# Output matrix in 8 KB runs of head pairs, and halves of a key pair joined ahead of the gather, in a decode step on one core

## The chip, the core and the metric

The kernel runs on one core of a Trainium2 chip. The core has a matrix engine (TensorE, PE in the profile, with PEld for its weight loads), a vector engine (DVE), a scalar engine (ACT), GpSimd (POOL) and a sync engine (SP) that issues nearly all of the loads. Sixteen DMA engines move data between HBM and the on-chip memory (SBUF). [...] The metric is device time of one execution in microseconds; the numbers of the profile come from one profiled execution.

## The reference

One decode step of a layer for 8 batch rows (B) of width 512 (D): a layer norm, attention with 32 query heads that share 8 key/value heads over the last 1024 positions of a 4096-long cache, and beside it a GELU-gated feed-forward of width 1792, whose silu gates the attention's output.

```python
xn = _layernorm(x)
q  = (xn @ wq)                                  # 32 heads of 128
k, v = last 1024 positions of the caches        # 8 heads, each for 4 query heads
scores = einsum("bhqd,bhkd->bhqk", q, k) * 128 ** -0.5
o  = einsum("bhqk,bhkd->bhqd", softmax(scores), v)
s  = o.reshape(B, 1, 4096) @ wo                 # the output matrix, 4096 x 512
g  = silu((gelu(xn @ w_gate) * (xn @ w_up)) @ w_down)
return x + s * g
```

All inputs are bf16. Keys and values of the window are 16 MB each, wq and wo 4 MB each, the feed-forward's three matrices 1.8 MB each: 47.5 MB in all.

## The kernel before, in words

**Loads.** Every large load goes through SP's queue into one pool of nine buffers of 2 MB (`big`, line 71): wq, the gate and up matrices, then keys (K) and values (V), a 2 MB tile for each of the 8 key heads, then the output matrix. `pending` (line 548) fixes the order K0 K1 K2, down, V0 K3 V1 K4 and so on to K7 V5 V6 V7; `fetch` issues them. A load waits on SP until PE has done with the buffer that it takes. `load_wo` (line 127) loads the output matrix in five pieces (lines 623 to 626): heads 0 to 3, heads 4 and 5, head 6, three quarters of head 7, the last quarter. Row `4p + r` of a head's 512 rows goes to partition p, so a head gives each partition one run of 4 rows, 4 KB.

**Sets.** A set is four batch rows of one key head: 16 sets (NS), two for each head (NB = 2). In a set each partition holds 32 consecutive keys of one batch row. The keys lie in pairs, and a pair (256 values in bf16) is turned as 128 four-byte words. For a set the kernel does, in order: `transpose_quarter` four times (four PE transposes each; one quarter is copied out by DVE, line 444, the next by ACT, line 446); `scores` (line 450), whose DVE step also finds each row's largest; `maxima` (line 471), a PE matmul into the columns `m_top` of a bank and a DVE step that makes the bias of the exponential; `exponentials` on ACT (line 485), which also sums; `turn` (line 496), a transpose on DVE; `value_half` twice (line 504); and for each head `gather` (line 520).

**The output of a set.** `value_half` multiplies 16 chunks of turned probabilities by pairs of values. Both keys of a pair meet the same weight columns, so the result (128 x 2 x 128, in the one bank of `ps_o`) holds for each row two halves, and only one of them is meant for it: `half` (line 261) says which. ACT copies both halves into `blk` (line 516), a 129th column of which holds the sum from the exponential; POOL copies that column for the second half (line 492). `gather(h)` sums over partitions with four PE matmuls for a head (two sets, two halves; the masks `sums`, lines 286 to 295, have `half` worked in) into the columns `m_out` of the bank that `m_top` also lies in, divides by the sum (DVE lines 531 and 533) and transposes the head into `oL` (line 541), the left operand of the projection. `project` (line 609) multiplies `oL` by the output matrix's rows, 16 matmuls a head, into one accumulator.

**The order.** The main loop (line 571) has two half-steps for a set, `t = 2s + i`. Each issues, for several sets at once: exponentials of set s-2, transposes of set s, the gather, more transposes, `turn` of s-2, scores or maxima of s-1, and a half of the values of the set nine half-steps behind. The engines take their instructions in this order, each from its own queue, so an instruction that waits holds up all behind it on that engine. The gather of head h comes at `i == 1` with `s = 6 + 2h`: after the first quarter's transposes, and ahead of that half-step's `maxima`. A set's values end at an even t, and its ACT copy comes at the end of that half-step. After the last gather come the 128 projection matmuls, in the order of the pieces, then two DVE steps and the two output DMAs.

Of the kernel before, what the change touches and what calls it, by code (L numbers as in the profile page):

```python
# [8 lines left out]
ACT = mybir.ActivationFunctionType  # L9
ALU = mybir.AluOpType  # L10
AX = mybir.AxisListType
BF16 = mybir.dt.bfloat16
FP32 = mybir.dt.float32
# [4 lines left out]
def kernel(  # L18
# [13 lines left out]
    nc = tc.nc  # L32

    B, Sq, D = A_x.shape
    Hkv, Sk, Dh = A_k_cache.shape[1], A_k_cache.shape[2], A_k_cache.shape[3]
    Hq = A_wq.shape[1] // Dh
    rep = Hq // Hkv
# [5 lines left out]
    scale = float(Dh) ** -0.5  # L43
    P = nc.NUM_PARTITIONS
# [6 lines left out]
    G = 4  # L51
    NB = B // G
# [4 lines left out]
    SET = NCH * Dh  # L57
# [3 lines left out]
    DP = Dh // 2  # L61
    NQB = D // 128
    PB = 32 // B

    NG = 2
    NS2 = NQB // NG
# [4 lines left out]
    big = ctx.enter_context(tc.tile_pool(name="big", bufs=9))  # L71
    kT_pool = ctx.enter_context(tc.tile_pool(name="kT_pool", bufs=2))
    p_pool = ctx.enter_context(tc.tile_pool(name="p_pool", bufs=2))
    consts = ctx.enter_context(tc.tile_pool(name="consts", bufs=1))
    small = ctx.enter_context(tc.tile_pool(name="small", bufs=3))
# [9 lines left out]


    m_ps = ps_m.tile([P, 512], FP32, name="m_ps")
    m_top, m_out = m_ps[:, 0:P], m_ps[:, P : P + Dh + 1]


    x_sb = rows.tile([B, D], BF16, name="x_sb")
# [23 lines left out]
                nc.sync.dma_start(out=t[:, y, :], in_=src[y])  # L115
        return [t[:, y, :].rearrange("p (c d) -> p c d", c=NCH) for y in range(NB)]

    HB = 2 * SET // (rep * D)
    wo_tiles = {}

    def wo_at(h):

        if h // HB not in wo_tiles:
            wo_tiles[h // HB] = big.tile([P, HB, rep * D], BF16, name="big")
        return wo_tiles[h // HB]

    def load_wo(h, r0, n, nh=1):

        t = wo_at(h)[:, h % HB : h % HB + nh, r0 * D : (r0 + n) * D]
        nc.sync.dma_start(  # L130
            out=t if nh > 1 else t[:, 0, :],
            in_=A_wo[h * rep * Dh : (h + nh) * rep * Dh, :].rearrange(
                "(h p r) n -> p h (r n)", p=P, r=rep
            )[:, :, r0 * D : (r0 + n) * D]
            if nh > 1
            else A_wo[h * rep * Dh : (h + 1) * rep * Dh, :].rearrange(
                "(p r) n -> p r n", r=rep
            )[:, r0 : r0 + n, :],
        )
        return [t[:, i, :].rearrange("p (r n) -> p r n", r=n) for i in range(nh)]  # L140

    wq_rows = []
    for k0, cuts in ((0, (1, 1)), (2, (2,))):
        t = big.tile([P, 2, Hq * Dh], BF16, name="big")
        i = 0
# [93 lines left out]
    quarter = consts.tile([P, NS2 + 32], FP32, name="quarter")  # L239
    nc.gpsimd.memset(quarter, 0.0)  # L240
    gsel = lead.tile([P, G], FP32, name="gsel")
    sums = consts.tile([P, 2, 2, rep, B, PB], FP32, name="sums")
    nc.gpsimd.memset(sums, 0.0)
    qT = qT0.rearrange("p (e s c g j) -> p e s c g j", e=2, c=2, g=G, j=rep)


    OW = 32
    OL = rep * OW
    oL = rows.tile([P, NS2 * (Hkv + 1), OL + 1], BF16, name="oL")
    nc.gpsimd.memset(oL, 0.0)  # L250

    def masks():
        nc.vector.tensor_reduce(
            out=parts, in_=identf.rearrange("p (x n) -> p n x", n=NC),
            axis=AX.X, op=ALU.max,
        )
        nc.vector.tensor_reduce(
            out=gsel, in_=parts.rearrange("p (g j) -> p g j", j=rep),
            axis=AX.X, op=ALU.max,
        )  # L260
        nc.vector.tensor_reduce(
            out=half, in_=identf.rearrange("p (r c n) -> p c r n", c=2, n=NC),
            axis=AX.XY, op=ALU.max,
        )
        nc.vector.tensor_reduce(
            out=quarter[:, NS2 : NS2 + B * NS2 : NS2],
            in_=identf.rearrange("p (a b f) -> p f b a", b=B, f=PB)[:, 0],
            axis=AX.X, op=ALU.max,
        )

        nc.vector.tensor_scalar(
            out=gsel, in0=gsel, scalar1=-1.0, scalar2=-NEG, op0=ALU.add, op1=ALU.mult
        )
        nc.vector.tensor_copy(
            out=own.rearrange("p c b g -> p (c b) g"),
            in_=gsel.unsqueeze(1).to_broadcast([P, CP * 32 // G, G]),
        )

        m = small.tile([P, NC], FP32, name="m16")
        nc.vector.tensor_scalar(  # L280
            out=m, in0=parts, scalar1=-1.0, scalar2=-NEG, op0=ALU.add, op1=ALU.mult
        )
        nc.vector.tensor_copy(
            out=same, in_=m.unsqueeze(1).to_broadcast([P, NR * 2, NC])
        )
        for c in range(2):
            for b in range(2):
                nc.vector.tensor_scalar(
                    out=sums[:, c, b].rearrange(
                        "p j (g y) f -> p y j g f", y=NB  # L290
                    )[:, b],
                    in0=parts.rearrange("p (g j) -> p j g", j=rep)
                    .unsqueeze(3).to_broadcast([P, rep, G, PB]),
                    scalar1=half[:, c : c + 1], scalar2=None, op0=ALU.mult,
                )

    hT = rows.tile([P, NFC, 32], BF16, name="hT")
# [7 lines left out]
    for k in range(NDC):  # L305
        w = wq_rows[k]
        for t in range(NT):
            for g in range(NQB):
# [3 lines left out]
                    w[:, 0, h * HD : (h + 1) * HD],  # L312
                    start=(k == 0), stop=(k == NDC - 1), skip_group_check=True,
                )
    q_row = rows.tile([P, NT, rep, 2, 2, DP], BF16, name="q_row")
    for c in range(2):
        nc.vector.tensor_copy(  # L317
            out=q_row[:, 0, :, :, c, :],
# [91 lines left out]

    def fold():

        f_sb = rows.tile([P, D], FP32, name="f_sb")
        nc.scalar.activation(out=f_sb, in_=f_state["ps"], func=ACT.Copy)
        spread(m_top, quarter, f_sb)
        f_state["ps"] = m_top[0 : 32 * NG]
# [66 lines left out]
        biases[s] = bias  # L483

    def exponentials(s):
        blk[s] = small.tile([P, 2, Dh + 1], FP32, name="blk", bufs=6)
        P_[s] = p_pool.tile([P, CP * 32], BF16, name="p")
        nc.scalar.activation(  # L488
            out=P_[s], in_=sc.pop(s), func=ACT.Exp, scale=scale, bias=biases.pop(s),
            accum_out=blk[s][:, 0, Dh : Dh + 1],  # L490
        )
        nc.gpsimd.tensor_copy(  # L492
            out=blk[s][:, 1, Dh : Dh + 1], in_=blk[s][:, 0, Dh : Dh + 1]
        )

    def turn(s):
# [2 lines left out]
            out=pT[s].rearrange("p c k -> p (c k)"), in_=P_.pop(s)  # L499
        )  # L500

    o_ps = {}

    def value_half(s, i):
        if i == 0:
            o_ps[s] = ps_o.tile([P, 2, Dh], FP32, name="o_ps")
        for c in range(i * CP // 2, (i + 1) * CP // 2):
            q = c % NR
            nc.tensor.matmul(  # L509
                o_ps[s][32 * q : 32 * q + 32].rearrange("p c d -> p (c d)"),  # L510
                pT[s][:, c, :],
                V[s][:, 2 * c : 2 * c + 2, :].rearrange("p c d -> p (c d)"),
                start=(c < NR), stop=(c >= CP - NR), skip_group_check=True,
            )
        if i == 1:
            nc.scalar.activation(out=blk[s][:, :, 0:Dh], in_=o_ps.pop(s), func=ACT.Copy)  # L516
            pT.pop(s)
            V.pop(s)

    def gather(h):  # L520

        ps = m_out
        for b in range(NB):
            t = blk.pop(h * NB + b)
            for c in range(2):
                nc.tensor.matmul(  # L526
                    ps, sums[:, c, b].rearrange("p j b f -> p (j b f)"), t[:, c, :],
                    start=(b == 0 and c == 0), stop=(b == NB - 1 and c == 1),
                )
        rec = small.tile([P, 1], FP32, name="rec")  # L530
        nc.vector.reciprocal(out=rec, in_=ps[:, Dh : Dh + 1])
        o = small.tile([P, rep, Dh // rep], BF16, name="o")
        nc.vector.tensor_scalar(
            out=o, in0=ps[:, 0:Dh].rearrange("p (i r) -> p r i", r=rep),
            scalar1=rec, scalar2=None, op0=ALU.mult,
        )


        out = oL[:, NS2 * h : NS2 * h + PB, 0:OL]
        out = out.rearrange("p f (r y) -> p r y f", y=OW)  # L540
        nc.vector.transpose(  # L541
            out=out[:, :, 0 : B * NS2 : NS2, :], in_=o.rearrange("p r i -> p (r i)")
        )


# [25 lines left out]
    for t in range(2 * NS + LV + 3):  # L571
# [3 lines left out]
        if s < NS:  # L575
            if i == 0 and s % NB == 0:
                fetch("K", s // NB)
            transpose_quarter(s, 2 * i)
        if i == 1 and s >= 6 and s % 2 == 0:
            gather((s - 6) // 2)  # L580
        if s < NS:
            transpose_quarter(s, 2 * i + 1)
        for _ in range(2):
# [22 lines left out]

    s_ps = ps_s.tile([32 * NG, 128], FP32, name="s")

    def project(h, r, w):
        t = oL[:, NS2 * h : NS2 * (h + 1)].rearrange("p f y -> p (f y)")  # L610
        for s in range(NS2):
            a = s * OL + r * OW
            for g in range(NG):
                q = NG * s + g
                nc.tensor.matmul(  # L615
                    s_ps[32 * g : 32 * g + 32, :], t[:, a : a + OW],
                    w[:, q * 128 : (q + 1) * 128],
                    start=(h == 0 and r == 0 and s == 0),
                    stop=(h == Hkv - 1 and r == rep - 1 and s == NS2 - 1),
                    skip_group_check=True,  # L620
                )

    pieces = [(0, 0, rep, 4), (4, 0, rep, 2), (6, 0, rep, 1)]

    pieces += [(Hkv - 1, 0, rep - 1, 1), (Hkv - 1, rep - 1, 1, 1)]
    for h0, r0, nr, nh in pieces:
        t = load_wo(h0, r0, nr, nh)
        for h in range(h0, h0 + nh):
            for r in range(r0, r0 + nr):
                project(h, r, t[h - h0][:, r - r0, :])  # L630
    tmp = small.tile([32 * NG, 128], FP32, name="tmp", bufs=1)
    out_sb = small.tile([32 * NG, 128], BF16, name="out_sb", bufs=1)
    nc.vector.tensor_tensor(out=tmp, in0=s_ps, in1=g_sb, op=ALU.mult)  # L633
# [36 lines left out]
```

## Time and profile before

| | |
|---|---|
| median of 3 runs | 120.56 us (120.37 to 120.61) |
| the profiled execution | 120.65 us, span 118.8 us |
| granted clock of TensorE, mean | 0.979 |
| busy: PE, PEld, DVE, ACT, POOL | 84.4, 59.2, 66.3, 56.2, 7.5 us |
| moved | 47.45 MB on queue q1; HBM read at 400 GB/s over the span |
| last gather on PE | 108.17 to 109.44 us |
| first, last projection matmul | 110.37, 115.67 us |
| the two DVE steps behind it, output DMAs issued | 115.71, 116.03; 116.34 us |

The span runs from the first instruction to the last. A busy share over the whole span mixes stretches with different limits; what a change is worth is read in the stretch that it touches, by what ends the waits there. A line of the order of time has the start, the time taken, the engine, the line of the kernel, the operation, what it writes and reads, how many were merged, and in brackets how long the engine had stood idle before and what ended that.

### The profile page before, as it was taken

The page shows a single profiled execution, that of the slowest core. Times are in us where ns is not written, and L with a number is a line of the kernel's source. Part 1 is how long each engine was busy: PE and PEld are TensorE (multiplying, and loading weights), DVE is VectorE, ACT ScalarE, POOL GpSimd, SP SyncE. Part 2 cuts the span into 40 slices and gives each one's busy share as a digit, 9 for nine tenths or more (in the row PEclk, how much of TensorE's full clock was granted, in tenths as well). Part 3 has the DMA queues.
Part 4 walks back from the last instruction along what each step waited for, and adds up shares of the span by engine and source line. Part 5 has one row for each costly group of instructions (what it writes and reads, how often), then busy time and mean ns, then how long its engine had stood idle before and what let it go on. Part 6 is the DMA issues. An engine that isn't in the chain of part 4 may idle for free.

```text
span 118.8 us, 2387 instructions
## 1 busy us (share of the span) xinstructions
PE 84.4 (71%) x974; PEld 59.2 (50%) x974; DVE 66.3 (56%) x171; ACT 56.2 (47%) x94; POOL 7.5 (6%) x28
## 2 busy tenths in 40 slices
PE   0070629599492999699969869787795988676670
PEld 0020216198262677377746557555573755555660
DVE  1310131837799766678848658585773965834301
ACT  0500030229808667575854884676565577132000
POOL 7700000000000000000000000000000000000000
PEclk9999999999999599999999999999999999999997
DMA  3999999999999999999999999999999999999940
GB/s 94 430 450 436 406 444 405 433 430 419 422 462 412 412 428 433 417 428 428 425 425 428 422 436 422 422 433 425 425 425 425 428 428 430 408 421 421 420 170 3
DMA packets 6569, 47.60 MB, mean 401 GB/s; under 512 B 536, under 2 KB 672, under 8 KB 1696
## 3 DMA queue, kind: packets, MB, share of 16 engines
q1 hardware_dynamic: 6512, 47.45, 95.2%
q8 instruction: 7, 0.11, 0.3%
q10 hardware_dynamic: 48, 0.01, 0.1%
q14 instruction: 2, 0.02, 0.0%
HBM read 47.46 MB, written 0.01 MB: 400 GB/s over the span
## 4 chain that ended last, share of the span: by engine, by line
DMA 86%; SPq 6%; PE 4%; issue 0%; DVE 0%
DMA big<-in_A_k_cache_dram 72%; DMA big<-in_A_wo_dram 14%; SPq L130 4%; PE kT_ps L433 3%; SPq L147 1%; SPq L98 1%; PE s L615 1%; PE sc L455 0%; DVE tmp L633 0%; DVE out_sb L634 0%; PE o_ps L509 0%
## 5 line engine op out<-in xcount | busy, mean ns | idle before, releaser
L446 ACT ACTIVATE kT<-kT_ps 128x1024 bf16<-128x1024 bf16 x32 | 32.5, 1021 | 23.6 <-PE kT_ps L433 23.5
L433 PE MATMUL kT_ps<-identf,big 128*128 128x128 f32 x256 | 38.5, 296 | 5.2 <-DMA big<-in_A_k_cache_dram 5.1
L433 PEld LDWEIGHTS kT_ps<-identf,big 128*128 128x128 f32 x256 | 30.9, 151 | 13.2 <-DMA big<-in_A_k_cache_dram 7.0
L444 DVE COPY kT<-kT_ps 128x1024 bf16<-128x1024 bf16 x32 | 22.0, 688 | 15.2 <-PE kT_ps L433 15.0
L488 ACT ACTIVATE p<-sc_sb,bias 128x512 bf16<-128x512 f32 x16 | 11.5, 717 | 7.0 <-DVE bias L479 6.5
L509 PE MATMUL o_ps<-big,pT 128*32 128x256 bf16 x256 | 12.3, 274 | 3.0 <-ACT blk L516 1.6
L498 DVE STREAM_TRANSPOSE pT<-p 128x512 bf16<-128x512 bf16 x16 | 11.3, 704 | 2.8 <-ACT p L488 2.8
L474 PE MATMUL m_ps<-identf,top 128*128 128x128 f32 x32 | 7.3, 309 | 6.0 <-DVE top L463 4.3
L463 DVE CUSTOM_DVE_ANT_0 sc_sb<-sc,own 128x512 f32<-128x512 f32 x16 | 10.5, 656 | 0.5 <-PE sc L455 0.5
L455 PE MATMUL sc<-kT,zeros 128*32 128x512 bf16 x128 | 10.3, 398 | 0.5 <-ACT kT L446 0.5
L509 PEld LDWEIGHTS <-pT 128*32 128x32 bf16 x256 | 5.8, 94 | 8.0 <-DMA big<-in_A_v_cache_dram 2.2
L526 PE MATMUL m_ps<-blk,sums 128*128 128x129 f32 x64 | 9.3, 286 | 0.0
L492 POOL COPY blk<-blk 128x1 f32<-128x1 f32 x16 | 2.9, 184 | 96.5 <-ACT p L488 92.2
L474 PEld LDWEIGHTS m_ps<-identf,top 128*128 128x128 f32 x32 | 4.8, 187 | 8.1 <-DVE top L463 5.0
L526 PEld LDWEIGHTS m_ps<-blk,sums 128*128 128x128 f32 x64 | 8.1, 191 | 0.9 <-issue 0.2
L516 ACT ACTIVATE blk<-o_ps 128x256 f32<-128x256 f32 x16 | 6.1, 381 | 3.0 <-PE o_ps L509 3.0
L541 DVE STREAM_TRANSPOSE oL<-o 128x128 bf16<-128x128 bf16 x8 | 6.0, 748 | 0.3
L310 PE MATMUL sc<-big,zeros 128*32 128x512 bf16 x16 | 2.5, 611 | 4.6 <-DMA big<-in_A_wq_dram 4.2
L615 PE MATMUL s<-big,oL 128*32 128x128 bf16 x128 | 4.3, 219 | 1.9 <-DMA big<-in_A_wo_dram 1.9
L317 DVE CAST q_row<-sc 128x512 bf16<-128x512 f32 x2 | 1.3, 686 | 7.8 <-PE sc L310 7.8
L615 PEld LDWEIGHTS <-oL 128*32 128x32 bf16 x128 | 3.8, 96 | 2.5 <-issue 2.3
L479 DVE CUSTOM_DVE_ANT_0 scr<-m_ps,same 128x128 f32<-128x128 f32 x16 | 4.9, 304 | 0.1
(70 smaller groups left out, 51.5 us busy)
## 6 DMA issues: line engine op xcount, KB each, us to landing
big<-in_A_k_cache_dram SPq DMA_DIRECT2D x7, 2048.0 KB, 34.1
big<-in_A_v_cache_dram SPq DMA_DIRECT2D x7, 2048.0 KB, 33.1
big<-in_A_wq_dram SPq DMA_DIRECT2D x2, 1024.0 KB, 5.8
big<-in_A_wq_dram SPq DMA_DIRECT2D x1, 2048.0 KB, 11.2
big<-in_A_k_cache_dram SPq DMA_DIRECT2D x2, 1024.0 KB, 21.3
big<-in_A_v_cache_dram SPq DMA_DIRECT2D x2, 1024.0 KB, 30.3
big<-in_A_wo_dram SPq DMA_DIRECT2D x1, 2048.0 KB, 30.9
big<-in_B_w_gate_dram SPq DMA_DIRECT2D x1, 1792.0 KB, 15.0
```

Source lines behind the costliest of these rows:

```text
L433: nc.tensor.transpose(ps[:, c, :], K[s][:, 2 * (i * QP + c) : 2 * (i * QP + c) + 2, :] .rearrange("p c d -> p (c d)").bitcast(FP32), identf,)
L444: nc.vector.tensor_copy(out=out, in_=in_)
L446: nc.scalar.activation(out=out, in_=in_, func=ACT.Copy)
L455: nc.tensor.matmul(ps[32 * R : 32 * R + 32], qT[:, e, s].rearrange("p c b j -> p (c b j)"), t[:, :, 32 * R : 32 * R + 32, e], start=(e == ...
L463: nc.vector.tensor_tensor_reduce(out=sc[s], in0=ps.rearrange("p c k -> p (c k)"), in1=own.rearrange("p c b g -> p (c b g)"), op0=ALU.add, ...
L474: nc.tensor.matmul(ps, top.pop(s).to_broadcast([P, P]), identf, start=True, stop=True)
L488: nc.scalar.activation(out=P_[s], in_=sc.pop(s), func=ACT.Exp, scale=scale, bias=biases.pop(s), accum_out=blk[s][:, 0, Dh : Dh + 1],)
L498: nc.vector.transpose(out=pT[s].rearrange("p c k -> p (c k)"), in_=P_.pop(s))
L509: nc.tensor.matmul(o_ps[s][32 * q : 32 * q + 32].rearrange("p c d -> p (c d)"), pT[s][:, c, :], V[s][:, 2 * c : 2 * c + 2, :].rearrange("p ...
L516: nc.scalar.activation(out=blk[s][:, :, 0:Dh], in_=o_ps.pop(s), func=ACT.Copy)
L526: nc.tensor.matmul(ps, sums[:, c, b].rearrange("p j b f -> p (j b f)"), t[:, c, :], start=(b == 0 and c == 0), stop=(b == NB - 1 and c == 1),)
L615: nc.tensor.matmul(s_ps[32 * g : 32 * g + 32, :], t[:, a : a + OW], w[:, q * 128 : (q + 1) * 128], start=(h == 0 and r == 0 and s == 0), s ...
```

## The change

Four things change together.

1. **The output matrix** is laid out by pairs of heads (m = 0 to 3) in place of heads. A pair's 1024 rows give each partition 8 consecutive rows, a run of 8 KB (`R8 = 8`). The five pieces keep their sizes: pairs 0 and 1, pair 2, half of pair 3, three of its rows, its last row. The first two move as runs of 8 KB, the others as runs of 4, 3 and 1 KB, as before.
2. **The join.** ACT copies only the first half of a set's output, scaled by the first column of `half`. Half a step later a new DVE instruction, `join`, adds the second half times the second column. `blk` has half the size, the POOL copy is gone, and the masks `sums` no longer hold `half`.
3. **The gather** moves to `i == 0` with `s = 7 + 2h`, one half-step later, behind the join of its second set, which now comes ahead of it. Its four matmuls have 64 columns of weights and put a head in half of the partitions; only every second gather goes on to the reciprocal, two scalings and one transpose, for two heads.
4. **Two banks.** The outputs of even sets (other than set 0) go to the bank of the pool `ps_s`, those of the others stay in `ps_o`.

The float copy of the down projection (`f_sb`) also takes the room of `q_row`.

```diff
+    R8 = 2 * rep
+    HB = 2 * SET // (R8 * D)
+    def load_wo(m, r0, n, nm=1):
+        t = wo_at(m)[:, m % HB : m % HB + nm, r0 * D : (r0 + n) * D]
+        src = A_wo.rearrange("(m p k) n -> p m (k n)", p=P, k=R8)
+        src = src[:, m : m + nm, r0 * D : (r0 + n) * D]
...
-        f_sb = rows.tile([P, D], FP32, name="f_sb")
+        f_sb = rows.tile([P, 2 * NT * HD], BF16, name="q_row")[:, 0 : 2 * D].bitcast(FP32)
...
-        blk[s] = small.tile([P, 2, Dh + 1], FP32, name="blk", bufs=6)
+        blk[s] = small.tile([P, Dh + 1], FP32, name="blk", bufs=7)
...
-        nc.gpsimd.tensor_copy(
-            out=blk[s][:, 1, Dh : Dh + 1], in_=blk[s][:, 0, Dh : Dh + 1]
...
+    def join():
+        s = joins.pop()
+        o = blk[s][:, 0:Dh]
+        nc.vector.scalar_tensor_tensor(
+            out=o, in0=o_ps.pop(s)[:, 1, :], scalar=half[:, 1:2], in1=o,
+            op0=ALU.mult, op1=ALU.add,
+        )
...
+            if s % 2 == 0 and s > 0:
+                o_ps[s] = ps_s.tile([P, 2, Dh], FP32, name="s")
+            else:
+                o_ps[s] = ps_o.tile([P, 2, Dh], FP32, name="o_ps")
...
-            nc.scalar.activation(out=blk[s][:, :, 0:Dh], in_=o_ps.pop(s), func=ACT.Copy)
+            nc.scalar.activation(
+                out=blk[s][:, 0:Dh], in_=o_ps[s][:, 0, :], func=ACT.Copy,
+                scale=half[:, 0:1],
+            )
+            joins.append(s)
...
     def gather(h):
+        x = h % 2
+        t = [blk.pop(h * NB + b) for b in range(NB)]
+        for a in range(2):
+            for b in range(NB):
                 nc.tensor.matmul(
+                    m_out[64 * x : 64 * x + 64, a, :],
+                    sums[:, b, a].rearrange("p j b f -> p (j b f)"), t[b],
+                    start=(b == 0), stop=(b == NB - 1), skip_group_check=True,
+                )
+        if x == 0:
+            return
+        rec = small.tile([P, 2], FP32, name="rec")
+        nc.vector.reciprocal(out=rec, in_=m_out[:, :, Dh])
+        o = small.tile([P, R8, 2, Dh // R8], BF16, name="o", bufs=2)
+        for a in range(2):
+            nc.vector.tensor_scalar(
+                out=o[:, :, a, :],
+                in0=m_out[:, a, 0:Dh].rearrange("p (i r) -> p r i", r=R8),
+                scalar1=rec[:, a : a + 1], scalar2=None, op0=ALU.mult,
+            )
...
-        if i == 1 and s >= 6 and s % 2 == 0:
-            gather((s - 6) // 2)
+        if joins:
+            join()
+        if i == 0 and s >= 7 and s % 2 == 1:
+            gather((s - 7) // 2)
...
-    pieces = [(0, 0, rep, 4), (4, 0, rep, 2), (6, 0, rep, 1)]
-    pieces += [(Hkv - 1, 0, rep - 1, 1), (Hkv - 1, rep - 1, 1, 1)]
+    last = Hkv // 2 - 1
+    pieces = [(0, 0, R8, 2), (2, 0, R8, 1)]
+    pieces += [(last, 0, rep, 1), (last, rep, rep - 1, 1), (last, R8 - 1, 1, 1)]
```

## The prediction

> **What bounds the kernel now.** I read the page's slices first, then the chain that ended last, then the same span cut into windows, then the tail of TensorE (PE) in order of time.
>
> ```profile
> span 118.8 us, 2387 instructions
> ...
> DMA  3999999999999999999999999999999999999940
> GB/s 94 430 450 436 406 444 405 433 430 419 422 462 412 412 428 433 417 428 428 425 425 428 422 436 422 422 433 425 425 425 425 428 428 430 408 421 421 420 170 3
> ...
> q1 hardware_dynamic: 6512, 47.45, 95.2%
> q8 instruction: 7, 0.11, 0.3%
> ...
> DMA 86%; SPq 6%; PE 4%; issue 0%; DVE 0%
> DMA big<-in_A_k_cache_dram 72%; DMA big<-in_A_wo_dram 14%; SPq L130 4%; PE kT_ps L433 3%; SPq L147 1%; SPq L98 1%; PE s L615 1%; PE sc L455 0%; DVE tmp L633 0%; DVE out_sb L634 0%; PE o_ps L509 0%
> ```
>
> The 16 DMA engines are full from the second slice to the thirty-eighth, and the chain is 86% DMA. Loads are issued some 30 us before they land, so a slip of a few us on PE, DVE or ACT starves no transfer. The last 4 MB are the output matrix. The windows (columns: length, busy of PE, PEld, DVE, ACT, POOL, clock, DMA share, GB/s) compare its stretch with the caches' and show the end:
>
> ```profile
> 75.00:85.00 10.00, 8.26 (x93) 6.01 (x94) 6.89 (x18) 6.38 (x11) 0.37 (x2) 1.00 1.01 426
> 85.00:95.00 10.00, 8.11 (x94) 5.85 (x93) 6.72 (x18) 6.20 (x11) 0.37 (x2) 1.00 1.01 426
> 105.50:111.50 6.00, 4.58 (x89) 3.88 (x90) 2.54 (x6) 1.09 (x3) 0.00 (x0) 1.00 1.03 422
> 113.00:114.00 1.00, 0.89 (x32) 0.75 (x27) 0.00 (x0) 0.00 (x0) 0.00 (x0) 1.00 0.81 306
> 114.00:115.00 1.00, 0.62 (x16) 0.48 (x16) 0.00 (x0) 0.00 (x0) 0.00 (x0) 1.00 0.37 138
> ```
>
> Runs of 8 KB move at 426 GB/s, runs of 4 KB at 422. From 113 on some DMA engines are done and others not. In the trace's records of single packets nine engines finish between 113.35 and 113.76, one near 114.2 and six at 114.89 to 115.01; the end hangs on those six.
>
> PE's tail, in order of time:
>
> ```profile
> 95.64 0.40 PE L509 MATMUL o_ps<-big,pT 128*32 128x256 bf16 x8 [0.39 <-DMA big<-in_A_v_cache_dram]
> ...
> 99.96 0.62 PE L455 MATMUL sc<-kT,zeros 128*32 128x512 bf16 x8 [0.53 <-ACT kT L446]
> ...
> 104.76 0.62 PE L509 MATMUL o_ps<-big,pT 128*32 128x256 bf16 x16 [1.08 <-ACT blk L516]
> 105.31 1.27 PE L526 MATMUL m_ps<-blk,sums 128*128 128x129 f32 x8
> 106.51 0.62 PE L509 MATMUL o_ps<-big,pT 128*32 128x256 bf16 x16
> 107.62 0.62 PE L509 MATMUL o_ps<-big,pT 128*32 128x256 bf16 x16 [0.49 <-ACT blk L516]
> 108.17 1.27 PE L526 MATMUL m_ps<-blk,sums 128*128 128x129 f32 x8
> ```
>
> 95.64 is the last time that PE waits for a cache tile on its normal path; from there to the end of the last gather (109.44) the order of the work sets the pace. The first 2 MB of the output matrix reach PE at 110.37, and the 128 projection matmuls then wait for DMA four times. This is the cover to watch.
>
> **The change part by part.**
>
> *Runs of 8 KB (the only term on the path).* The pieces stay at 2, 1, 0.5, 0.375 and 0.125 MB, with the same number of DMAs in the same places of SP's queue. Only the first two change: 3 MB in 384 packets instead of 768. Per DMA engine that is 24 packets of 8 KB for 48 of 4 KB. In the packet records an engine takes 4.90 us for 2 MB of cache and 4.97 us for the first 2 MB of the output matrix, and 2.49 against 2.45 for the next 1 MB: 0.11 us. The windows give 3.146 MB at 422 against 426 GB/s, 0.07 us. The packets' own durations (309 ns against twice 159) would give 24 x 9 = 0.22 us, but they overlap, so that is the outer bound. I take -0.10, the mean of the two that measure progress; bounds -0.22 and 0 (rates equal). SP issues fewer descriptors; its wait in that queue lies 6 us and more ahead of the need.
>
> *POOL's 16 copies* (184 ns) vanish; POOL is idle. *ACT's eviction* goes from 128x256 (381 ns, 16 of them) to 128x128 with a scale: between the 128x32 copy (256) and 381; I take 310, near the 64x128 Tanh's 271. ACT frees 1.1 us, off the path.
>
> *The join* is new on DVE, 16 times: between the 64x128 add from PSUM (283) and the 128x128 scale from PSUM (351); I take 320, or 5.1 us in all. Against it the work behind the gather goes from 8 x (168 + 351 + 748) = 10.1 us to 4 x (168 + 2 x 351 + 748) = 6.5 us. Net +1.5 us on a DVE that is 56% busy: hidden under DMA.
>
> *Gather:* still 8 matmul instructions a head; PE moves on 0.89 us (93.06 to 93.95) to 1.20 us (105.31 to 106.51) later. With 64 columns of weights I bound it by half of 0.89 and by 1.20. *Setup:* four mask products (248 ns) become smaller copies; POOL's memsets of 515 and 2030 ns change by about -0.26 and +0.22 and end near 5.2 us, before anything reads them. f_sb in q_row's room waits for reads done by 21 us; fold comes at 49. All 0.
>
> *The two moves: where the cover could go.* The gather of head h leaves the second half-step before DVE's maxima and goes to the first half-step after the join; the outputs of even sets get bank s. Until 95.64 the DMA resets the clock: PE waits 1.24 us for the last keys at 90.77 and 0.39 at 95.64, and one gather (0.89) passes from the second wait's side to the first's. From 95.64 I laid the new order out by hand, each engine in its own order, starts spaced as in the trace. Gather 4 now stands behind 95.64: scores of the last set start at 100.82 instead of 99.96. Its top comes at 102.80, join 11 and the bias at 103.76. Gather 5 runs at 103.64 and is done by 104.91 (1.27); DVE then does reciprocal, two scalings and a transpose (0.20 + 0.38 + 0.38 + 0.55) and is free at 106.46. Only then it turns the last probabilities (to 107.10) and joins sets 12 and 13 (to 107.74); set 14 waits for set 12's bank until 107.5, and gather 6 for join 13 until 107.83. PE follows: gather 6 to 109.03, second half of set 14, set 15 from 109.36 to 109.98, eviction to 110.33, join 15 to 110.73; the six matmuls of gather 7 behind it end at 111.7. That is with the dear gather; with 0.89 three times, 110.9. So the last gather ends 1.5 to 2.3 us later than 109.44, although two waits on ACT (1.08 and 0.49) are gone.
>
> What does it cost? PE does a projection matmul each 27.5 ns; the 112 before the fourth piece's end need 3.1 us, and that piece's rows reach PE at 115.05 - 0.10 = 114.95 (its 12 and the last 4 follow as now). PE may start projecting as late as about 111.85. The last pair's rows of oL are ready by 111.7 + 1.8 = 113.5, needed at 114.0. So the delay fits, with 0.1 to 0.9 us to spare: cost 0, bounds 0 and +0.4 (below).
>
> Sum against the profiled execution: 120.65 (span 118.8, 1.85 around it) - 0.10 = 120.55. It stood 0.09 above the median of the runs (120.56), so for a median: 120.46, say 120.45.
>
> **The rivals.**
>
> *PE's tail becomes the end (slower).* Place: gather 7, behind joins 12 to 15 that queue on DVE behind gather 5's scalings. It decides once gather 7 ends after 111.85. If each join takes 380 ns of DVE and each scaling into 16-element runs 450, I count 0.45 later than 111.7: 112.2, and an end 0.35 late: 120.45 + 0.35 = 120.8; with one more unseen wait of 0.5, 121.3. For it: the margin is smaller than the shift. Against: the 111.7 has the dear gather already.
>
> *The runs don't matter.* The end is on six engines that are late for another reason, and their lateness stays; if 4 KB and 8 KB packets go equally fast on them, the time is 120.56. Against: those six show the same 4.97 as the others.
>
> *An instruction fetch falls on a late engine.* Each of the six late engines was hit by one 16 KB instruction packet (30.7, 47.5, 60.6, 74.4, 87.1, 100.5; the page's q8), which put it some 1.4 us back; 8 KB ones at 40.3 and 65.8 put theirs 0.84 and 0.55 back. DVE gets 8 instructions more. If that brings one more 8 KB fetch and it hits one of the six, the end moves by 0.55 to 0.84: 121.0 to 121.3. PE's count is the same, so I expect the same seven.
> [...]
>
> **How the numbers follow.** 0.2% (0.24 us, below 120.32 or above 120.80) is about what a measurement of this kernel can tell from no change. Forecast (only DMA's term): 0.60, of it 0.10 below 120.32 with the outer bound and the runs' scatter (120.37 to 120.61). Runs don't matter: 0.10, all within. PE's tail: 0.20, of it 0.13 above 120.80. Fetch: 0.05, all above. A gain of some 0.3 us that I don't see, from a late engine that is spared: 0.05. Faster 0.15, same 0.67, slower 0.18. The range for 8 in 10 is 120.2 to 121.0; the forecast's own is 120.3 to 120.6.
>
> **What would show it.** Right: GB/s near 426 instead of 422 while the first 3 MB of the output matrix move; six DMA engines still late; the last gather between 110.5 and 111.8, and the matmuls of pieces three to five still waiting for DMA. Wrong: no DMA wait in front of the last 32 projection matmuls (PE's tail); join or scaling over 0.4 us; the last packet later than 115.0 with gaps or a further fetch in it; GB/s unchanged.

## The result, and the profile after

| | before | after |
|---|---|---|
| median of 11 runs each | 120.56 us (120.37 to 120.66) | 121.77 us (120.68 to 122.89) |
| ratio, 95% interval | | 1.0093 (1.0075 to 1.011) |
| the profiled execution | 120.65 us, span 118.8 | 121.77 us, span 119.8 |
| last gather on PE | 108.17 to 109.44 us | 110.77 to 113.03 us |
| first, last projection matmul | 110.37, 115.67 us | 112.95, 116.70 us |
| output DMAs issued | 116.34 us | 117.38 us |
| last packet of the output matrix | 115.01 us | 114.74 us |
| busy: PE, DVE, ACT, POOL | 84.4, 66.3, 56.2, 7.5 us | 83.6, 68.8, 55.7, 4.6 us |

The change makes the kernel slower, by 0.93%. The range on record (120.2 to 121.0) misses the time. The runs also scatter over 2.2 us, where those of before lie within 0.3. The ratios, here and below, rest on the runs within 1.5% of a kernel's fastest one, so they leave out the two longest here (122.75 and 122.89), four of run 5 and one of run 6, and need not equal the quotient of the medians.

The page of the changed kernel, slices, queues and chain:

```profile
span 119.8 us, 2373 instructions
...
PEclk9999999959997699999999999999999999997699
DMA  4999999999999999999999999999999999999910
GB/s 109 416 440 437 446 402 433 424 432 421 427 452 422 409 427 432 413 429 435 427 427 416 427 432 432 408 432 432 432 429 410 429 429 435 410 432 419 382 42 3
...
q8 instruction: 7, 0.11, 0.3%
...
DMA 71%; PE 15%; DVE 5%; ACT 4%; SPq 2%; issue 1%
```

The DMA engines are as full as before, up to the same slice. But the chain has lost 15 points of DMA and gained 11 of PE and 5 of DVE: the end no longer hangs on a transfer. And the clock line, which the forecast did not use for PE's tail, shows 7 and 6 in the slices from 108 to 114 us. PE's tail in order of time:

```profile
95.42 0.40 PE L516 MATMUL s<-big,pT 128*32 128x256 bf16 x8 [0.48 <-DMA big<-in_A_v_cache_dram]
...
103.85 1.09 PE L538 MATMUL m_ps<-blk,sums 128*64 128x129 f32 x8
104.87 0.40 PE L516 MATMUL s<-big,pT 128*32 128x256 bf16 x8
105.10 0.61 PE L516 MATMUL o_ps<-big,pT 128*32 128x256 bf16 x16
107.94 0.40 PE L516 MATMUL s<-big,pT 128*32 128x256 bf16 x8 [2.23 <-DVE blk L502]
108.27 1.09 PE L538 MATMUL m_ps<-blk,sums 128*64 128x129 f32 x8
109.30 0.62 PE L516 MATMUL s<-big,pT 128*32 128x256 bf16 x8
109.70 1.07 PE L516 MATMUL o_ps<-big,pT 128*32 128x256 bf16 x16
110.77 0.69 PE L538 MATMUL m_ps<-blk,sums 128*64 128x129 f32 x2
111.63 1.40 PE L538 MATMUL m_ps<-blk,sums 128*64 128x129 f32 x6 [0.16 <-DVE blk L502]
112.95 3.75 PE L635 MATMUL s<-big,oL 128*32 128x128 bf16 x128
```

The last line is the verdict: 128 projection matmuls in one row, with no DMA wait ahead of any. All of the output matrix that they need is there first, and PE's tail sets the end. Two things above it made it late. PE stood idle for 2.23 us ahead of set 14, for a join (`blk` L502). And the 16 matmuls of set 15 took 1.07 us where the same 16 at 105.10 took 0.61. What DVE did in the 2.23 us:

```profile
104.98 0.17 DVE L546 RECIPROCAL rec<-m_ps 128x2 f32<-128x2 f32 x1 [1.19 <-PE m_ps L538]
105.18 0.61 DVE L549 TENSOR_SCALAR o<-m_ps,rec 128x128 bf16<-128x128 f32 x2
105.83 1.31 DVE L559 STREAM_TRANSPOSE oL<-o 128x256 bf16<-128x256 bf16 x1
106.77 0.89 DVE L493 STREAM_TRANSPOSE pT<-p 128x512 bf16<-128x512 bf16 x1
107.58 0.31 DVE L502 SCALAR_TENSOR_TENSOR blk<-s,half,blk 128x128 f32<-128x128 f32 x1
107.81 0.33 DVE L502 SCALAR_TENSOR_TENSOR blk<-o_ps,half,blk 128x128 f32<-128x128 f32 x1
```

Durations of neighbours overlap, so the distance of the starts is what counts. The transpose of the pair into `oL` holds DVE for 0.94 us (105.83 to 106.77), the turn behind it for 0.81 (to 107.58). The joins that PE waits for stand behind both. The same two steps before, 0.55 us (102.62 to 103.17) for one head and 0.64 (100.64 to 101.28) for the turn:

```profile
100.64 0.71 DVE L498 STREAM_TRANSPOSE pT<-p 128x512 bf16<-128x512 bf16 x1 [1.20 <-ACT p L488]
101.28 0.65 DVE L463 CUSTOM_DVE_ANT_0 sc_sb<-sc,own 128x512 f32<-128x512 f32 x1
...
102.62 0.75 DVE L541 STREAM_TRANSPOSE oL<-o 128x128 bf16<-128x128 bf16 x1
103.17 0.32 DVE L479 CUSTOM_DVE_ANT_0 scr<-m_ps,same 128x128 f32<-128x128 f32 x1
```

Windows of the changed kernel. The clock changed at 109.32 and 112.74, 3.41 us apart; the last three are cut near there and at steps of 3.4 us back from there (columns as in the prediction):

```profile
75.00:85.00 10.00, 8.47 (x96) 6.12 (x95) 7.07 (x20) 7.25 (x12) 0.00 (x0) 1.00 1.02 428
105.50:111.50 6.00, 3.73 (x50) 2.05 (x42) 3.24 (x8) 1.29 (x4) 0.00 (x0) 0.82 1.00 421
...
102.50:105.90 3.40, 2.68 (x42) 1.91 (x43) 1.82 (x9) 1.32 (x4) 0.00 (x0) 1.00 1.00 424
105.90:109.30 3.40, 1.36 (x18) 0.97 (x17) 2.24 (x4) 0.23 (x1) 0.00 (x0) 1.00 1.00 424
109.30:112.72 3.42, 3.25 (x32) 2.14 (x32) 0.70 (x2) 0.73 (x2) 0.00 (x0) 0.50 1.00 417
```

PE was busy for 1.36 of 3.40 us, and then the granted clock was 0.50 for the next 3.42 us. Before, it was 1.00 from 100 to 117 us.

### The profile page after: what moved, and what is told of

It is laid out like the page before. It is cut to its first block, busy times and chain, and to the rows that moved or that the text cites. A ratio compares the mean times of both kernels' runs of the same rounds, so it can differ in the third digit from the quotient of the medians.

```text
span 119.8 us, 2373 instructions
## 1 busy us (share of the span) xinstructions
PE 83.6 (70%) x974; PEld 58.5 (49%) x974; DVE 68.8 (57%) x179; ACT 55.7 (46%) x94; POOL 4.6 (4%) x12
## 4 chain that ended last, share of the span: by engine, by line
DMA 71%; PE 15%; DVE 5%; ACT 4%; SPq 2%; issue 1%
DMA big<-in_A_v_cache_dram 53%; DMA big<-in_A_k_cache_dram 17%; PE kT_ps L431 5%; PE m_ps L538 4%; PE s L635 3%; ACT kT L444 1%; PE s L516 1%; DVE oL L559 1%; ACT L376 1%; DVE pT L493 1%; SPq L145 1%; SPq L99 1%; PE o_ps L516 1%; ACT p L486 1%; DVE o L549 1%
## 5 line engine op out<-in xcount | busy, mean ns | idle before, releaser
L431 PE MATMUL kT_ps<-identf,big 128*128 128x128 f32 x256 | 37.9, 293 | 1.6 <-DMA big<-in_A_k_cache_dram 1.5
L431 PEld LDWEIGHTS kT_ps<-identf,big 128*128 128x128 f32 x256 | 30.0, 149 | 9.6 <-issue 2.6
L516 PE MATMUL s<-big,pT 128*32 128x256 bf16 x112 | 5.8, 283 | 7.3 <-DMA big<-in_A_v_cache_dram 5.1
L538 PE MATMUL m_ps<-blk,sums 128*64 128x129 f32 x64 | 9.7, 296 | 0.2 <-DVE blk L502 0.2
L538 PEld LDWEIGHTS m_ps<-blk,sums 128*64 128x64 f32 x64 | 7.4, 146 | 2.4 <-DVE blk L502 1.1
L516 PE MATMUL o_ps<-big,pT 128*32 128x256 bf16 x144 | 7.5, 290 | 0.4 <-DVE blk L502 0.4
L559 DVE STREAM_TRANSPOSE oL<-o 128x256 bf16<-128x256 bf16 x4 | 5.3, 1328 | 0.2
L318 ACT ACTIVATE q_row<-o_ps 128x512 bf16<-128x512 f32 x2 | 1.1, 594 | 8.5 <-PE o_ps L305 8.5
L524 ACT ACTIVATE blk<-s,half 128x128 f32<-128x128 f32 x7 | 2.5, 363 | 4.5 <-PE s L516 4.5
L305 PEld LDWEIGHTS <-zeros 128*32 128x32 bf16 x32 | 1.1, 120 | 7.2 <-issue 6.7
```

Source lines behind the costliest of these rows:

```text
L431: nc.tensor.transpose(ps[:, c, :], K[s][:, 2 * (i * QP + c) : 2 * (i * QP + c) + 2, :] .rearrange("p c d -> p (c d)").bitcast(FP32), identf,)
L516: nc.tensor.matmul(o_ps[s][32 * q : 32 * q + 32].rearrange("p c d -> p (c d)"), pT[s][:, c, :], V[s][:, 2 * c : 2 * c + 2, :].rearrange("p ...
L538: nc.tensor.matmul(m_out[64 * x : 64 * x + 64, a, :], sums[:, b, a].rearrange("p j b f -> p (j b f)"), t[b], start=(b == 0), stop=(b == NB ...
L559: nc.vector.transpose(out=out[:, :, 0 : B * NS2 : NS2, :], in_=o.rearrange("p r a d -> p (r a d)"))
```

## The experiments

Two theories stood at the start. **Order**: DVE's work behind a pair's gather (reciprocal, two scalings, one long transpose) stands ahead of the turn and the joins that PE waits for. **Clock**: the idle stretch makes the clock fall to half, and set 15 and the last gather run slowly. The rivals to both were the 8 KB runs, the gather's place half a step later, and the projection's length itself. Runs 1 to 4 shared one chip and its 24 runs of before (120.69), runs 5 to 8 another (25 runs, 120.65).

| run | median us (range), runs | ratio to before (95%) |
|---|---|---|
| 1 8 KB runs alone | 120.58 (120.33 to 120.70), 11 | 0.9993 (0.9984 to 1.0001) |
| 2 half of the projection | 122.22 (121.78 to 122.71), 4 | 1.0135 (1.0107 to 1.0162) |
| 3 DVE's order | 120.70 (120.48 to 120.93), 12 | 1.0007 (0.9998 to 1.0017) |
| 4 filler on PE | 121.13 (120.96 to 122.32), 5 | 1.007 (1.0037 to 1.0104) |
| 5 gather as early as before | 121.96 (120.52 to 122.88), 10 | 1.006 (1.0031 to 1.009) |
| 6 one bank | 126.29 (124.90 to 126.86), 4 | 1.0426 (1.0372 to 1.0481) |
| 7 order, and the gather early | 120.75 (120.47 to 120.96), 11 | 1.0009 (1.0001 to 1.0018) |
| 8 filler twice | 120.89 (120.65 to 121.34), 8 | 1.0024 (1.001 to 1.0038) |

**1. The 8 KB runs alone, in the kernel before.** The loads are those of the change; heads, joins and gathers stay.

```diff
-    pieces = [(0, 0, rep, 4), (4, 0, rep, 2), (6, 0, rep, 1)]
+    pieces = [(0, 0, R8, 2), (2, 0, R8, 1)]
...
+                project(2 * m + k // rep, k % rep, t[m - m0][:, k - r0, :])
```

> The kernel before with one part of the change: the output matrix is loaded by pairs of heads (first two pieces in 8 KB runs). The projection multiplies the same number of rows in another order than the left operand has, so the product is not the reference's; the work is the same. Theory T (the tail of PE made the change slow, the runs did what was forecast): 120.46 us, 0.10 below before, the first 2 MB in 4.90 us instead of 4.97 on a DMA engine. Rival D (the 8 KB runs bring nothing, or cost): 120.56 or more.

Measured: 0.9993, or -0.08 us, against -0.10 forecast; the interval reaches from -0.19 to +0.01. In the packet records a DMA engine took 4.90 us for the first 2 MB of the output matrix (4.97 before), as it does in the changed kernel, whose next 1 MB took 2.46 (2.49 before). The runs cost nothing that shows; the loss lies elsewhere. The interval just includes zero, so the time alone does not tell a gain of 0.1 us from none; the packet records do show the higher rate. DMA sets the end of this kernel too: its projection waits for the output matrix four times (0.90, 0.49, 0.21 and 0.32 us). Of its runs, one at a mean clock of 0.928 took 120.70 and one at 0.942 took 120.49, beside 120.67 at 0.979 and 120.41 at 0.980: in these runs a lower mean clock does not show in the time.

**2. The changed kernel with half of the projection.**

```diff
-        for m in range(m0, m0 + nm):
+        for m in range(max(m0, 2), m0 + nm):
```

> The changed kernel without the 64 projection matmuls of pairs 0 and 1 (their part of the result is left out; the loads stay). Theory T: the end is PE, which starts to project at 112.95 and needs 27.5 ns a matmul; 64 fewer take 1.76 us, until DMA's end takes over (last packet at 114.74, then 0.36 to PE and 0.3 of matmuls, against 116.7 now): 1.2 us less than the changed kernel, about 120.5, and a scatter as small as before's. Rival C (the loss is a lower clock all along the run, not the tail): it stays above 121.2.

Measured: not shorter; the ratio, 1.0135, is above the changed kernel's 1.0093. Its profiled run (122.53) had two stretches at half clock in the tail, and its end looks like this:

```profile
114.06 1.07 PE L635 MATMUL s<-big,oL 128*32 128x128 bf16 x32
116.38 1.07 PE L635 MATMUL s<-big,oL 128*32 128x128 bf16 x32 [1.25 <-DVE oL L559]
```

64 matmuls less, and PE waits for the last pair's rows of `oL`: 2.3 us from the end of gather 7 through reciprocal, scalings and transpose, and 32 matmuls behind, together 3.3 us from 114.13 against 3.75 for all 128. So behind a late gather 7 stands a second path that is only some 0.4 us shorter. The expectation missed that path. So half of the projection could save no more than those 0.4 us, and the four runs, at mean clocks of 0.926 to 0.957, do not show them. What the profile does show is that the end follows gather 7, which ended at 114.13 here and at 113.03 in the changed kernel's profile. The windows of this run, cut at its clock changes:

```profile
99.98:103.39 3.41, 1.65 (x28) 0.86 (x26) 2.27 (x8) 2.08 (x4) 0.00 (x0) 1.00 1.01 420
103.39:106.80 3.41, 3.41 (x34) 2.32 (x36) 0.94 (x5) 0.92 (x3) 0.00 (x0) 0.50 1.01 428
106.80:110.21 3.41, 1.53 (x31) 1.11 (x20) 2.45 (x5) 0.63 (x2) 0.00 (x0) 1.00 1.02 430
110.21:113.62 3.41, 3.24 (x32) 1.81 (x31) 0.70 (x2) 0.74 (x2) 0.00 (x0) 0.50 0.94 384
```

PE is busy for 1.65 and for 1.53 of 3.41 us, and both times the clock is 0.50 in the next 3.41. The instructions up to here are those of the changed kernel; but counted in steps of 3.41 us from the changes of its clock, its windows begin at 102.50 and 105.90, these at 103.39 and 106.80, and the idle stretches fall into them otherwise.

**3. The changed kernel with DVE's order mended.** Reciprocal and scalings go behind the turn, and the transpose into `oL` three half-steps later, behind the joins.

```diff
-        if x == 0:
-            return
+        if x == 1:
+            scales.append(h)
...
             turn(s - 2)
+        if scales:
+            scale_pair()
+            flip_at = t + 3
...
+        if flips and t == flip_at:
+            flip_pair()
```

> The changed kernel with DVE's part of the gather moved back in DVE's queue: reciprocal and scalings behind the turn of the probabilities, the transpose into oL three half-steps later. Theory T: joins 12 and 13 come by 106.7 instead of 107.9, PE's idle stretch of 2.2 us shrinks under 1 us, the last gather ends by 111.0, no half-clock window falls into the tail, DMA is the end again: 120.45 to 120.6, scatter under 0.4. Rival C: clock windows stay, 121.2 or more. A third possibility, the earlier half-steps suffer from the transposes' new place: gather 7 later than 111.8 although the joins are early.

Measured: 1.0007, level with before (120.70, 0.1 us above the band expected, with 120.69 for before on this chip). DVE and PE in order of time:

```profile
104.86 0.71 DVE L493 STREAM_TRANSPOSE pT<-p 128x512 bf16<-128x512 bf16 x1 [0.94 <-ACT p L486]
105.50 0.13 DVE L551 RECIPROCAL rec<-m_ps 128x2 f32<-128x2 f32 x1
105.67 0.61 DVE L554 TENSOR_SCALAR o<-m_ps,rec 128x128 bf16<-128x128 f32 x2
106.19 0.34 DVE L502 SCALAR_TENSOR_TENSOR blk<-s,half,blk 128x128 f32<-128x128 f32 x1
```

```profile
106.58 0.40 PE L516 MATMUL s<-big,pT 128*32 128x256 bf16 x8 [0.75 <-DVE blk L502]
...
109.20 1.31 PE L538 MATMUL m_ps<-blk,sums 128*64 128x129 f32 x8 [0.42 <-DVE blk L502]
110.44 1.96 PE L649 MATMUL s<-big,oL 128*32 128x128 bf16 x64
112.68 1.07 PE L649 MATMUL s<-big,oL 128*32 128x128 bf16 x32 [0.27 <-DMA big<-in_A_wo_dram]
```

The wait for the join falls from 2.23 to 0.75 us, the clock is 1.00 from 98.00 to 116.00, gather 7 ends at 110.51 instead of 113.03, and the waits for the output matrix are back. Nothing but the order of four DVE instructions a pair was changed: all of the loss that shows hangs on that order.

**4. The changed kernel with work for PE in the idle stretch.** Ten matmuls of 512 columns, whose result nothing reads, stand ahead of set 14; DVE's order stays.

```diff
             value_half(s3, i3)
+        if t == LV + 2 * 13 + 1:
+            fill = ps_kT.tile([P, 512], FP32, name="kT_ps")
+            for j in range(10):
+                nc.tensor.matmul(
+                    fill[0:32, :], ident[:, 0:32],
+                    pT[14].rearrange("p c k -> p (c k)"), start=True, stop=True,
+                )
```

> The changed kernel with ten matmuls of 512 columns put into PE's idle stretch before set 14 (results unused), everything else as it is. Theory T in its second part (the idle stretch of 2.2 us is what halves the clock in the next 3.4 us window): no window at 0.5 between 108 and 113, set 15's values in 0.6 us and the last gather in 1.1; 120.7 to 120.9, with the order's share of the loss left. Rival C (the clock falls for another reason): 121.4 to 122.3 as now, window still there.

Measured: 1.007, a median of 121.13 where 120.7 to 120.9 was expected, with two of the five runs at 121.89 and 122.32. In its profiled run (121.06) the clock was 1.00 from 101.20 to 111.45, and the projection behind it took as long as the changed kernel's at full clock, 3.75 us:

```profile
106.03 2.32 PE L628 MATMUL kT_ps<-pT,ident 128*32 128x512 bf16 x10
...
111.05 1.31 PE L538 MATMUL m_ps<-blk,sums 128*64 128x129 f32 x8 [0.42 <-DVE blk L502]
112.29 3.75 PE L642 MATMUL s<-big,oL 128*32 128x128 bf16 x128
```

The profile gives the share of each cause. From set 14's first matmul to the end of gather 7 it takes 3.92 us here (108.44 to 112.36), and 5.09 in the changed kernel's profile (107.94 to 113.03): half clock cost the changed kernel's profiled run 1.17 us. But the projection still waits for no DMA: the order alone makes PE the end. The two long runs were not profiled. If the clock fell in them, one filler does not keep it up in every execution.

**5. The changed kernel with the gather as early as before.**

```diff
-        if i == 0 and s >= 7 and s % 2 == 1:
-            gather((s - 7) // 2)
+        if i == 1 and s >= 6 and s % 2 == 0:
+            gather((s - 6) // 2)
```

> The changed kernel with one part undone: the gather goes back to the half-step that it had before (i == 1, s = 6 + 2h), still behind its join. Theory T: gather 4 leaves the stretch behind the last wait for values, but the pair's scalings and transpose (1.76 us of DVE) come ahead of the bias again and PE waits for the join in front of the gather; last gather near 111.5, 120.7 to 121.3, between before and the changed kernel. If the half-step alone were the loss: as before, 120.5. If it had no part in it: 121.8.

Measured: a median of 121.96 over runs from 120.52 to 122.88, the same scatter; 120.7 to 121.3 was expected, and the 121.8 on record stood for a half-step without any part in the loss. So the half-step is not the loss by itself. The profiled run is the one of 120.52. Its clock was 1.00 from 102.50 to 112.72, although PE waited 1.91 us for a join:

```profile
107.70 1.13 PE L538 MATMUL m_ps<-blk,sums 128*64 128x129 f32 x8 [1.91 <-DVE blk L502]
...
111.48 4.03 PE L635 MATMUL s<-big,oL 128*32 128x128 bf16 x128
```

One kernel gives 120.52 and 122.88. That the longer runs are those whose clock fell fits runs 2, 4 and 8, but of this kernel only the shortest was profiled. The mean clocks do not settle it: a run of 122.00 has 0.972, the one of 120.52 has 0.971.

**6. The changed kernel with one bank for the outputs.**

```diff
-            if s % 2 == 0 and s > 0:
-                o_ps[s] = ps_s.tile([P, 2, Dh], FP32, name="s")
-            else:
+            if True:
                 o_ps[s] = ps_o.tile([P, 2, Dh], FP32, name="o_ps")
```

> The changed kernel with one part undone: all sets' outputs in the one bank of ps_o. Theory T: in the tail set 13 must wait for join 12, set 14 for join 13 and set 15 for join 14, each behind an eviction of 0.37 and a join of 0.35 us; the last gather later by 1.5 to 3 us than 113.0, 123 to 125 us, so that the second bank is not what cost time but hides a part of the join. Rival (the second bank makes the wait of set 14): 121.2 or less.

Measured: 1.0426, a median of 126.29 and more than expected. PE's waits for a join are 2.67, 0.84 and 0.86 us in its profile, and the projection begins at 117.60. Its matmuls also ran at about half speed in between (gather 6 took 1.98 us at 110.83, gather 5 1.09 at 104.31), so the time is not that of the waits alone. Without the second bank the kernel is slower still, so the bank is no part of the loss; with the join on DVE it is needed (126.29 us without it, 121.77 with it), since a bank now comes free only behind DVE's queue, as those three waits show.

**7. Order mended, and the gather half a step earlier, behind the maxima.** DVE's part is moved back as in run 3; the cut shows the gather alone.

```diff
-        if i == 0 and s >= 7 and s % 2 == 1:
-            gather((s - 7) // 2)
...
             maxima(s - 1)
+        if i == 1 and s >= 6 and s % 2 == 0:
+            gather((s - 6) // 2)
```

> The changed kernel with DVE's part of the gather moved back as in the run with the new DVE order, and the gather's matmuls a half-step earlier, behind that half-step's maxima (so ahead of the last wait for values). Theory T: last gather at 109.3 to 110, two us and more of cover, DMA is the end whatever the clock does: what the 8 KB runs bring is left, 0.1 us under before (ratio 0.999), scatter as before's. Rival (the rest of the change costs something off the tail too): ratio 1.000 or more.

Measured: 1.0009 (1.0001 to 1.0018), where 0.999 was expected. Gather 7 ends at 109.71, within 0.3 us of the kernel before, and PE waits for each piece of the output matrix (0.92, 0.39, 0.24, 0.31 us). With the cover whole again, the ratio is still 0.16% above that of run 1, on the side of the rival on record, that the rest of the change costs something off the tail. The last packet lands at 115.20 in its profile, at 115.11 in run 1's, 114.89 in run 3's and 114.74 in the changed kernel's: it differs by some tenths from profile to profile, and no run shows what moves it. Whether the 0.16% is that, or a small cost of the rest, is not settled.

**8. The changed kernel with two fillers**, five matmuls more ahead of the last maxima.

```diff
+        if t == LV + 2 * 11 + 1:
...
+            for j in range(5):
...
+        if t == LV + 2 * 13 + 1:
...
+            for j in range(10):
```

> The changed kernel with five matmuls of 512 columns in PE's idle stretch before the last maxima and ten in the one before set 14 (results unused). If a window of 3.41 us in which PE is busy less than half (1.7 us) is what makes the next one run at half clock: no such window can come between 99 and 113 in any phase, so the scatter falls to 0.4 us and the time to 120.8 to 121.1, the order's share alone. If the clock falls for another reason: times up to 122.3 and a median over 121.3.

Measured: 1.0024, a median of 120.89 as expected. The scatter is down to 0.69 us (120.65 to 121.34), where 0.4 was expected; the two longest runs, 121.31 and 121.34, were not profiled. In its profile PE is busy for at least 2.74 us of each window of 3.4 us from 93.70 to 110.78, and the clock is 1.00 in all of them:

```profile
105.87 2.32 PE L635 MATMUL kT_ps<-pT,ident 128*32 128x512 bf16 x10
...
112.13 3.78 PE L649 MATMUL s<-big,oL 128*32 128x128 bf16 x128
```

With the fillers, which go with a whole clock in the profiled run, DVE's order costs 0.24%, about 0.3 us over before. The rest of the changed kernel's 0.93%, some 0.8 us, and most of the scatter (2.21 us, now 0.69) went with them.

## Why the prediction was wrong

**Right: the runs.** -0.10 was forecast, run 1 alone gives -0.08 with an interval of 0.2. The sign forecast for it, GB/s near 426 in the window from 105.5 to 111.5, shows in run 1 (425) and not in the changed kernel (421). Windows are too coarse for it: the caches' 8 KB runs alone read 428 and 422 in two neighbouring windows of the changed kernel (75 to 85 and 85 to 95). The packet records are the better reading, and there it shows in both.

**Right, and without weight:** POOL's copies, the smaller masks, `f_sb`, the join's size (320 taken, 340 measured), the gather's (PE moves on 1.02 us behind its start at full clock, 103.85 to 104.87, between the bounds). ACT's eviction was taken at 310 ns and measured 364: half the columns, now with a scale, saved 17 ns of 381. The instruction fetches stayed at seven (q8 of both pages) and six engines stayed late, as expected: in the packet records their last packets end between 114.62 and 114.75.

**Wrong, the term that was mis-sized: the transpose for two heads.** It was priced as the old one, 0.55 us of DVE, though it has twice the elements. The only row for it was that of 128x128, and neither "the same" nor "twice" was given as a bound. The groups of the changed kernel:

```profile
L559 DVE STREAM_TRANSPOSE oL<-o 128x256 bf16<-128x256 bf16 x4 | 5.3, 1328 | 0.2
L502 DVE SCALAR_TENSOR_TENSOR blk<-o_ps,half,blk 128x128 f32<-128x128 f32 x9 | 3.1, 342 | 0.5 <-ACT blk L524 0.5
L524 ACT ACTIVATE blk<-o_ps,half 128x128 f32<-128x128 f32 x9 | 3.3, 364 | 0.8 <-PE o_ps L516 0.7
```

1328 ns against 748, and 0.94 us of DVE against 0.55: +0.39 in front of the joins. The turn behind it took 0.81 instead of 0.64: +0.17. In sum DVE was busy for 2.5 us more than before (68.8 against 66.3), where +1.5 was forecast.

Counted from the landing of the last values that PE waits for, set 14 was to start after 11.86 us (95.64 to 107.5) and started after 12.52 (95.42 to 107.94). Of these 0.66 us, 0.25 stood already at the end of gather 5 (9.27 forecast, 9.52 measured), so the layout by hand ran short ahead of the transpose as well; scalings and join gave 0.15 back. From set 14 to the end of gather 7 the forecast had 4.20 us, and run 4 took 3.92 at full clock. Together gather 7 was to end 16.06 us behind the landing (95.64 to 111.7). At full clock, in run 4, it took 16.44 (95.92 to 112.36); the forecast itself allowed 16.21 (up to 111.85). So the step "so the delay fits, with 0.1 to 0.9 us to spare" fails already here, by 0.23.

The projection was priced rightly: the first 112 of its matmuls took 3.14 us in runs 4 and 8 (3.1 taken). In run 8's profile, at full clock, the last one ends at 115.91, 0.34 behind the 115.57 that the forecast stands for (115.67 before, less 0.10). Of that, 0.23 is the step above, and 0.12 that the same stretch began at 95.76 instead of 95.64. The time was 120.89, against the 120.55 forecast for a profiled execution. The last pair's rows of `oL`, taken as ready 1.8 us behind gather 7, were late too: in run 2 the matmuls that need them start 2.25 us behind it (114.13 to 116.38).

**Wrong, the term that was left out: the clock.** The working laid out PE's tail with durations at full clock and by its own times put an idle stretch of about 2 us in it (gather 5 done at 104.91, some 0.6 us of set 13 behind it, set 14 at 107.5), without asking what that does to the clock. The page of before has a clock line, and it has a dip:

```profile
PEclk9999999999999599999999999999999999999997
```

It was 0.50 from 38.62 to 42.03, behind 3.41 us in which PE was busy for 0.86.

In the profile of the changed kernel, gather 7 ended 17.61 us behind that landing (95.42 to 113.03), and 1.17 of the 1.55 us above the forecast are half clock.

**The rivals.** "PE's tail becomes the end" is what happened; it had 0.20. Its place, its point of decision (gather 7 after 111.85) and its sign (no DMA wait ahead of the last 32 projection matmuls) were right. Its mechanism was not: joins at 380 and scalings at 450 ns did not come (342 and 347). Its price, 120.8 to 121.3, was too low, since it knew no clock.

**The range** should have held the rival's case with an unknown of its own. A margin of 0.1 us on a path laid out by hand over 16 us, with one row stretched to a shape that the trace did not show, was given 0.67 for "same".

## What to carry to other kernels

Where a change merges two small instructions into a larger one on an engine that takes its queue in order, bound the new size by the old duration and by twice it (here 748 ns became 1328), and look at who stands behind it in that queue: here the longer transpose and the turn behind it put 0.56 us in front of a wait, and another order of the same instructions cut that wait from 2.23 to 0.75 us (run 3). On a kernel bound by DMA, lay out the other engines' tail with its slack to the last transfers, and treat a slack below the sum of the unknowns as an even chance. And when a change opens an idle stretch on PE, read the granted clock behind it: here it was 0.50, and 16 matmuls took 1.07 us instead of 0.61, in a kernel whose runs scatter over 2.2 us.

## What was not expected of the hardware

**Half clock came behind stretches in which PE stood idle for half of the time or more.** In the clock records of the profiles of before and after, a stretch of one clock lasts 3.41, 6.83, 10.24, 68.27 or 75.09 us: 1, 2, 3, 20 and 22 times 3.413 (the last one of each, which ends behind the kernel, left out). The windows here are steps of 3.41 us, counted from the changes of the clock. Those with a clock of 0.50 behind them:

| profile | window | PE busy, us | clock behind it |
|---|---|---|---|
| before | 35.21 to 38.62 | 0.86 | 0.50 |
| before | 113.71 to 117.12, last matmul in it | 1.43 | 0.50 |
| after | 20.58 to 23.99 | 1.19 | 0.50 |
| after | 34.23 to 37.64 | 0.98 | 0.50 |
| after | 105.90 to 109.30 | 1.36 | 0.50 |
| after | 116.15 to 119.56, last matmul in it | 0.56 | 0.50 |

In all other windows of the two profiles, from the first clock record (28.38 and 20.58 us) to the window of the last matmul, PE was busy for 1.95 us or more, and the clock behind each was 1.00. In run 2, windows with 1.65 and 1.53 us were followed by 0.50. Run 5 kept the whole clock behind one with 1.61:

```profile
105.90:109.31 3.41, 1.61 (x28) 1.36 (x32) 1.20 (x3) 1.28 (x4) 0.00 (x0) 1.00 1.03 437
109.31:112.72 3.41, 2.99 (x72) 2.29 (x65) 1.76 (x6) 0.73 (x2) 0.00 (x0) 1.00 0.98 408
```

So the clock stayed whole behind 1.61 us in one profile and fell behind 1.65 in another: these runs show no sharp limit, nor what sets it. In the changed kernel's profile an idle stretch of 2.23 us, 2.04 of it in one window, came ahead of the fall; with ten matmuls in its place the clock was 1.00 there (run 4).

**The same kernel, then, has several times.** An idle stretch lies within one window in one execution and over two in another. PE's wait of 1.20 us ahead of the last maxima lies over two windows in the changed kernel's profile (101.77 to 102.97, with the edge at 102.50; PE busy for 2.13 and 2.68 us), and the clock stays at 1.00. In run 2's it lies in one (101.88 to 103.08, before the edge at 103.39; 1.65 us), and the next window is at 0.50. That such differences are what spreads the changed kernel from 120.68 to 122.89 us is an inference: the fillers of run 8 took most of the spread away (0.69 us were left of 2.21), and of the changed kernel's eleven runs the fastest has the highest mean clock (0.971, the others 0.940 to 0.957), but only one of the eleven was profiled. In run 1, with DMA at the end, 120.70 us at a mean clock of 0.928 stand beside 120.67 at 0.979.

**The time of a DVE transpose differed with its shape and its output.** 128x512 from the exponentials takes 0.71 us, 128x128 into `oL` 0.75, 128x256 into `oL` 1.33. The two into `oL` write with a stride, the first does not; that the stride is the cause was not tested.
